# The inverse norms of q leave for DRAM in runs of 128 bytes, the planner's times for DRAM trips are set anew, and squares and scores may also use other pairs of a chunk

## The chip, the cores and the metric

The kernel runs on one core of one Trainium2 chip. The metric is the time of the whole program on the device, in microseconds: 2173.47 us as the median of three runs (2170.49 to 2175.32). TensorE (PE) multiplies matrices, VectorE (DVE), ScalarE (ACT) and GpSimd (POOL) work on elements, SyncE (SP) issues all DMAs from one queue.

## The reference

```python
# B, N, C = 4, 6080, 256; d_ff = 2048; all float32
qn = q / (np.linalg.norm(q, axis=1, keepdims=True) + 1e-6)     # over the 6080 tokens
kn = k / (np.linalg.norm(k, axis=1, keepdims=True) + 1e-6)
s = kn.transpose(0, 2, 1) @ qn / tau                           # 256 x 256 per batch
a = softmax(s, -1)                                             # sum + 1e-9
x = (v @ a).reshape(B * N, C)
h = x @ w_in
g = h * (1.0 / (1.0 + np.exp(-1.702 * h)))
out = g @ w_out
```

## The kernel before

Attention over channels needs only a 256 x 256 matrix per batch, and it is folded into the first weights: `a.T`-weighted `w_in` is made once per batch, and v goes through it directly. Float32 products are made of three matmuls with operands split into a high and a low part (ACT copies the high part, DVE subtracts to get the low one).

The main work is cut into 4 batches x 6 chunks of 1024 tokens (one chunk of each batch has 960) x 8 pairs of 128-wide feature blocks, 192 pairs in all. A pair (`lay`) has seven products `m1` to `m7` into `ps_x`, `ps_y`, `ps_z` (L818), copies and sums on ACT and DVE (L852 to L861), the gate on ACT (L872), its high and low parts (L877, L881), and the second product into `ps_o` (L894).

Beside the pairs of batch b runs the attention of batch b + 1, in small jobs. For each unit of 2 x 128 tokens a `score_job` loads q and k, splits them (L308, L313), multiplies (L388), sums on DVE (L406) and squares and adds for the norms (L321 on ACT, L333 on POOL). A `square_job` only loads again and squares: the four units of batch 1 whose scores were made at the start need it. When all units are done, `softmax_job` runs one chain:

- `norms_blocks`, `norms_part` (DVE, L413, L417), then to DRAM and back with channels on partitions (`part_rows`, L423; `quarters`, L429);
- `norms_sum`, `norms_root` (POOL), `norms_b` (DVE): the inverse norms `rn`, 128 x 4, q in the first two columns;
- q's two columns to DRAM as a row `q_row` (L445), and the row back, broadcast to 128 partitions, as `rq` (L452);
- `softmax_a` (DVE, L500, L504): x from sums, rn and rq, and its extreme; the exponential on ACT (L509); the scaling, a transposition and a trip through DRAM that turns x (`turned`, L533; `whole`, named `mixed` in the trace, L539); then the products with `w_in` (`fold`, L610) and the splitting of the new weights (L702, L704), which the first pair of batch b + 1 needs.

The order on every engine is set while the program is built. A planner goes through the pairs with its own clock (a matmul triple is 1.0 of its units, which is 0.68 us). It keeps for each token the time at which it is ready, and gives a job's step a place on its engine once what it needs is ready by that clock. A DMA costs nothing on SP; its `wait=` is the time until its data count as there. So `wait=` decides behind how much other work the reader of the data stands in its engine's queue. Each engine then runs its own list in order and waits on semaphores: an instruction whose data are late holds up all behind it.

Of the kernel before, what the change touches and what calls it, by code (L numbers as in the profile page):

```python
# [11 lines left out]
F32 = mybir.dt.float32  # L12
# [7 lines left out]
P = 128  # L20
# [8 lines left out]
def channel_attention_then_glu(  # L29
# [23 lines left out]
    nc = tc.nc  # L53
    B, N, C = q.shape
    DFF = w_in.shape[1] // 2
    NC2 = C // P
# [25 lines left out]
    small = ctx.enter_context(tc.tile_pool(name="small", bufs=1))  # L82
# [116 lines left out]
    class Attention:  # L199
# [223 lines left out]
            nc.sync.dma_start(self.part_rows, self.part_sums)  # L423

        def norms_in(self):
            self.quarters = small.tile([P, 2 * NC2, P // 32], F32, tag="quarters", name="quarters")
            src = self.part_rows.rearrange("(a u) (n b) -> b u n a", u=32, b=P // 32)
            for b in range(P // 32):
                nc.sync.dma_start(self.quarters[32 * b : 32 * b + 32], src[b])  # L429

        def norms_sum(self):
            self.rn = small.tile([P, 2 * NC2], F32, tag="rn", name="rn")
            nc.vector.tensor_reduce(self.rn, self.quarters, axis=AX.X, op=ALU.add)

        def norms_root(self):
# [2 lines left out]
        def norms_b(self):  # L438
            rn = self.rn
            nc.vector.tensor_scalar_add(rn, rn, 1e-6)  # L440
            nc.vector.reciprocal(rn, rn)

        def norms_q_out(self):
            self.q_row = dram.tile([1, C], F32, name=f"q_row{self.b}")
            nc.sync.dma_start(self.q_row.rearrange("o (n p) -> p (o n)", p=P), self.rn[:, :NC2])  # L445

        def norms_k(self):
            nc.vector.tensor_scalar_mul(self.rn[:, NC2:], self.rn[:, NC2:], rtau)
# [258 lines left out]
    whole = {}  # L707
# [96 lines left out]
    class Hidden:  # L804
# [54 lines left out]
        def add(self, out, a, z):  # L859
            out, a, z = (getattr(self, t) for t in (out, a, z))  # L860
            nc.vector.tensor_tensor(out, a, z, op=ALU.add)  # L861
# [65 lines left out]
    PAIRS = NF // 2  # L927
# [442 lines left out]
    def turn(tag, token, releases, deep=2):  # L1370
        ring = rings.setdefault(tag, [])
        deps = list(ring[-deep][1]) if len(ring) >= deep else []
        if ring and ring[-1][0] != token:
            deps.append(ring[-1][0])
        ring.append((token, releases))
        return deps
# [88 lines left out]
    def mix_room(s):  # L1465
        for n in range(4):
            mix_rooms[s, n] = turn("words", ("mix", s, n, "load"), [("mix", s, n, "keep")])
# [58 lines left out]
    def v_job(b, c, due, begin):  # L1526
        job = Job(due, begin)
        key = ("v", b, c)
        pair = (b * NCHUNK + c) * PAIRS
        for second in range(2):  # L1530
            low = ((*key, "px"), (*key, "py")) if not second else ((*key, "pw"), (*key, "pz1"))
            room = turn("words", (*key, second), [low[0], (*key, second, "+", 1)])
            room += turn("words", (*key, second), [low[1], *([(*key, "pz0")] if second else [])])
            job.add("SP", 0, (*key, second), room, v_load, b, c, second, wait=6.0 if b or c > 1 else 9.5)
            for n in range(3 if second else 2):
                deps = [(*key, second, "+", n - 1)] if n else [(*key, second)]
                job.add(
                    *(("DVE", 1.15) if (b, c) == (0, 1) else ("POOL", 2.2)),
                    (*key, second, "+", n), deps, v_sum, b, c, second, n,
                )  # L1540
            last = [(*key, second, "+", 2 if second else 1)]
            if second:
                job = Job(due - 0.5, begin)
                maker[*key, "late"] = job
                parts = (("pw", None, 1.0, 1.15), ("pz", 0, 1.0, 1.15), ("pz", 1, 1.0, 1.15))
            else:
                parts = (("px", None, 1.65, 1.9), ("py", None, 1.65, 1.9))
            for tag, n, da, dd in parts:
                name = tag if n is None else f"{tag}{n}"
                deps = list(last)  # L1550
                if second and (b or c):
                    deps += [("m4" if tag == "pw" else "m3", pair - 1)]
                if tag in ("px", "py") and (b, c) == (0, 1):
                    deps += [("s1", 7)]
                if not second and (b, c) >= (0, 2):
                    deps += [("m6", pair - PAIRS - 1)]
                job.add("ACT", da, (*key, name, 0), deps, v_part, b, c, tag, n, False)
                job.add("DVE", dd, (*key, name), [(*key, name, 0)], v_part, b, c, tag, n, True)
# [56 lines left out]
    def softmax_job(b, begin):  # L1615
        A = ats[b]
        job = Job(begin + 3, begin)
        key = ("soft", b)

        def add(eng, dur, name, deps, fn, *a, **kw):  # L1620
            job.add(eng, dur, (*key, name), deps, fn, *a, **kw)

        last = [summed[b, i] for i in range(2)]
        room = turn("sq", (*key, "blocks"), [(*key, "part")])
        add("DVE", 1.05, "blocks", [*last, *room], A.norms_blocks)
        add("DVE", 1.05, "part", [(*key, "blocks")], A.norms_part)
        job.add("SP", 0, (*key, "out"), [(*key, "part")], A.norms_out, wait=3.5)
        job.add("SP", 0, (*key, "in"), [(*key, "out")], A.norms_in, wait=5.0)
        add("DVE", 0.3, "sum", [(*key, "in")], A.norms_sum)
        add("POOL", 1.5, "root", [(*key, "sum")], A.norms_root)  # L1630
        add("DVE", 0.6, "b", [(*key, "root")], A.norms_b)
        job.add("SP", 0, (*key, "qo"), [(*key, "b")], A.norms_q_out, wait=3.5)
        add("DVE", 0.3, "k", [(*key, "b")], A.norms_k)
        room = turn("sq", (*key, "q"), [(*key, "x")])
        job.add("SP", 0, (*key, "q"), [(*key, "qo"), *room], A.norms_q, wait=3.5)
        room = turn("qs", (*key, "x0"), [(*key, "out2")])
        add("DVE", 1.6, "x0", [(*key, "q"), ("sums", b, len(A.units)), *room], A.softmax_a, 0)
        add("DVE", 1.6, "x", [(*key, "x0")], A.softmax_a, 1)
        maker[*key, "exp"] = job
        add("ACT", 5.8, "exp", [(*key, "x")], A.softmax_b)  # L1640
        add("DVE", 1.8, "c", [(*key, "exp")], A.softmax_c)
        add("DVE", 1.05, "tblocks", [(*key, "c")], A.turn_blocks)
        job.add("SP", 0, (*key, "out2"), [(*key, "tblocks")], A.turn_out, wait=5.0)
        room = turn("qs", (*key, "whole"), [("mixed", b)])
        job.add("SP", 0, (*key, "whole"), [(*key, "out2"), *room], A.turn_in, wait=4.0)
        add("ACT", 1.0, "turn", [(*key, "whole")], A.turned)
        job.add("DVE", 1.15, ("turned", b), [(*key, "turn")], A.turned_low)
        for n in range(4):
            add("DVE", 0.45, ("mix", n), [(*key, ("mix", n - 1)) if n else ("turned", b)], A.mixed, n)
        used = [("fold", b, NG // 2 - 1, len(FOLD) - 2)]  # L1650
        room = turn("sq", (*key, ("mix", "h")), used) + turn("sq", (*key, ("mix", "h")), used)
        add("ACT", 1.0, ("mix", "h"), [(*key, ("mix", 3)), *room], A.mixed_split, False)
        job.add("DVE", 1.15, ("mixed", b), [(*key, ("mix", "h"))], A.mixed_split, True)
# [160 lines left out]
    for b in range(B):  # L1814
        for c in range(NCHUNK):
            if b or c:
                p = (b * NCHUNK + c) * PAIRS
                v_job(b, c, p - (4 if b else 1), p - 5)
            if b == 0 and c in MIX_AT:
                mix_room(MIX_AT.index(c))  # L1820
        if b + 1 < B:
            o = b * NCHUNK * PAIRS
            u, last_u = ats[b + 1].direct, len(ats[b + 1].units)
            again = list(range(u))
            for p in range(3 if b else PAIRS + 1, TOTAL):
                if b == 0 and p % PAIRS == 0 and p // PAIRS in MIX_AT:
                    mix_job(MIX_AT.index(p // PAIRS), p)
                if p % PAIRS == 5 and again or u == last_u:
                    square_job(b + 1, again.pop(0), o + p)
                elif p % PAIRS not in (0, 5):  # L1830
                    score_job(b + 1, u, o + p)
                    u += 1
                    if u == last_u:
                        half_job(Job(o + p + 2, o + p + 1), b + 1, u, [])
                if u == last_u and not again:
                    break
            softmax_job(b + 1, o + p)
            for h in range(NG // 2):
                weight_job(b + 1, h, o + NCHUNK * PAIRS - PAIRS + (-4, 1)[h])
# [42 lines left out]
```

## Time and profile before

| | us |
|---|---|
| median of three runs | 2173.47 |
| the profiled execution | 2173.61 |
| its span | 2171.8 |
| PE busy | 2148.0 (99%) |
| ACT busy | 1543.3 (71%) |
| DVE busy | 1328.0 (61%) |
| POOL busy | 439.0 (20%) |

The span is what the trace covers; 1.8 us of the execution lie around it. Matmuls overlap in the records: one of 128x512 lasts 0.39 us, and the next starts 0.227 us after it when the granted clock is full.

### The profile page before, as it was taken

To read this page: it belongs to the slowest core of one execution; us is meant where nothing else is said; L and a number is where in the kernel's file an instruction comes from. 1 tells how busy PE (TensorE), PEld (TensorE's weight loads), DVE (VectorE), ACT (ScalarE), POOL (GpSimd) and SP (SyncE) were. 2 spreads that over 40 slices of the span, in tenths; PEclk is the share of its full clock that TensorE was granted. 3 is DMA by queue.
4 is the path that set the end of the run, shared out by engine and by line. 5 is a ranking of instruction groups with operands and counts; after the bars stand their busy time and mean duration, and the time that the engine had idled before them with its cause. 6 is when DMAs were issued, how large, how long until landed. Compare 5 with 4: busy or idle time off the path is not lost.

```text
span 2171.8 us, 26774 instructions
## 1 busy us (share of the span) xinstructions
PE 2148.0 (99%) x9654; PEld 1791.5 (82%) x9654; DVE 1328.0 (61%) x1996; ACT 1543.3 (71%) x2740; POOL 439.0 (20%) x465
## 2 busy tenths in 40 slices
PE   9999999999999999998999999999899999999999
PEld 8888888887888888887888888888788888888887
DVE  7986656656666666665566666666556644544443
ACT  7987777776677777775667777777566766666665
POOL 0003234231212423321121332242112100100100
PEclk9999999999999999999999999999999999999999
DMA  9433334212322222221222212121222110110100
GB/s 368 163 108 92 122 97 155 92 42 69 107 86 88 63 78 63 85 66 45 93 88 85 81 59 78 49 90 61 51 88 87 59 39 20 59 39 20 56 20 19
DMA packets 104757, 175.46 MB, mean 81 GB/s; under 512 B 22832, under 2 KB 31664, under 8 KB 104624
## 3 DMA queue, kind: packets, MB, share of 16 engines
q1 hardware_dynamic: 104624, 173.76, 24.5%
q8 instruction: 75, 1.23, 0.2%
q14 instruction: 58, 0.48, 0.1%
HBM read 137.52 MB, written 36.20 MB: 80 GB/s over the span
## 4 chain that ended last, share of the span: by engine, by line
PE 94%; DMA 3%; ACT 1%; DVE 1%; issue 0%; SPq 0%; POOL 0%; DVEq 0%; ACTq 0%
PE ps_o L894 46%; PE ps_x L818 23%; PE ps_z L818 11%; PE ps_y L818 6%; PE s L388 4%; PE s L349 2%; PE ps_w L610 1%; DMA q_row<-rn 1%; DMA rq<-q_row 1%; DMA words<-in_w_in 0%; PE ps_w L663 0%; DMA part_rows<-part 0%; DVE gl L881 0%; DVE r L861 0%; DMA quarters<-part_rows 0%
## 5 line engine op out<-in xcount | busy, mean ns | idle before, releaser
L894 PE MATMUL ps_o<-gh,wo_l 128*128 128x512 f32 (+1 forms) x1536 | 596.2, 388 | 0.0
L894 PE MATMUL ps_o<-gh,wo_h 128*128 128x512 f32 (+1 forms) x1536 | 596.2, 388 | 0.0
L894 PE MATMUL ps_o<-gl,wo_h 128*128 128x512 f32 (+1 forms) x1536 | 472.0, 388 | 0.8 <-DVE gl L881 0.8
L881 DVE TENSOR_TENSOR gl<-g,gh 128x512 fp32r<-128x512 f32 (+1 forms) x384 | 273.9, 753 | 145.1 <-ACT gh L877 144.9
L894 PEld LDWEIGHTS ps_o<-gl,wo_h 128*128 128x128 f32 x1536 | 289.0, 188 | 58.8 <-DVE gl L881 1.2
L894 PEld LDWEIGHTS ps_o<-gh,wo_h 128*128 128x128 f32 x1536 | 289.2, 188 | 57.9
L894 PEld LDWEIGHTS ps_o<-gh,wo_l 128*128 128x128 f32 x1536 | 289.1, 188 | 57.6
L333 POOL TENSOR_TENSOR acc<-acc,sq 128x256 f32<-128x256 f32 x276 | 219.3, 801 | 521.8 <-ACT sq L321 510.9
L818 PE MATMUL ps_x<-vh,wh 128*128 128x512 f32 (+1 forms) x768 | 300.4, 391 | 16.6 <-DVE r L861 15.9
L881 DVE TENSOR_TENSOR gl<-ps_y,gh 128x512 fp32r<-128x512 f32 (+1 forms) x192 | 131.7, 686 | 294.3 <-ACT gh L877 293.8
L818 PE MATMUL ps_x<-vl,wh 128*128 128x512 f32 (+1 forms) x768 | 299.0, 389 | 0.0
L818 PE MATMUL ps_x<-vh,wl 128*128 128x512 f32 (+1 forms) x768 | 298.1, 388 | 0.0
L783 POOL TENSOR_TENSOR v_raw<-v_raw 128x512 f32<-128x512 f32 (+1 forms) x110 | 159.8, 1461 | 633.4 <-DMA v_raw<-in_vT 365.0
L872 ACT ACTIVATE r<-r 128x512 f32<-128x512 f32 (+1 forms) x192 | 120.5, 628 | 191.4 <-DVE r L861 191.4
L852 ACT COPY r<-ps_x 128x512 f32<-128x512 f32 (+1 forms) x189 | 110.3, 583 | 178.6 <-PE ps_x L818 178.5
L877 ACT CAST gh<-g 128x512 fp32r<-128x512 f32 (+1 forms) x384 | 216.4, 613 | 0.1
L881 DVE TENSOR_TENSOR gl<-r,gh 128x512 fp32r<-128x512 f32 (+1 forms) x192 | 146.9, 765 | 66.7 <-ACT gh L877 63.7
L818 PEld LDWEIGHTS ps_x<-vh,wh 128*128 128x128 f32 x768 | 145.1, 189 | 47.1 <-DVE r L861 17.7
L852 ACT COPY r<-ps_z 128x512 f32<-128x512 f32 (+1 forms) x192 | 111.9, 583 | 80.2 <-PE ps_z L818 80.2
L818 PEld LDWEIGHTS ps_x<-vh,wl 128*128 128x128 f32 x768 | 144.9, 189 | 29.1
L818 PEld LDWEIGHTS ps_x<-vl,wh 128*128 128x128 f32 x768 | 145.2, 189 | 25.8
L406 DVE TENSOR_TENSOR sums<-sums,s 128x256 f32<-128x256 f32 x138 | 58.0, 420 | 153.6 <-PE s L388 151.2
(145 smaller groups left out, 3304.0 us busy)
## 6 DMA issues: line engine op xcount, KB each, us to landing
v_raw<-in_vT SPq DMA_DIRECT2D x80, 512.0 KB, 4.6
out_T<-osb SPq DMA_DIRECT2D x80, 256.0 KB, 2.0
raw_q<-in_q SPq DMA_DIRECT2D x74, 256.0 KB, 2.7
raw_k<-in_k SPq DMA_DIRECT2D x74, 256.0 KB, 2.7
fold<-t SPq DMA_DIRECT2D x48, 256.0 KB, 2.8
fold<-b SPq DMA_DIRECT2D x36, 256.0 KB, 2.9
v_raw<-in_vT SPq DMA_DIRECT2D x16, 480.0 KB, 3.9
words<-in_w_in SPq DMA_DIRECT2D x8, 512.0 KB, 5.4
```

Of the source, the lines that this page charges most:

```text
L333: nc.gpsimd.tensor_tensor(acc, acc, sq[:, j, :], op=ALU.add)
L349: nc.tensor.matmul(self.s[:, i, :], lhsT=lhsT, rhs=rhs, start=self.first, stop=last, skip_group_check=True,)
L388: nc.tensor.matmul(out, lhsT=ks[:, j, low, ci], rhs=rhs, start=n == 0, stop=n == len(terms) - 1, skip_group_check=True,)
L406: nc.vector.tensor_tensor(out, out, part, op=ALU.add)
L610: nc.tensor.matmul(self.ps, lhsT=l, rhs=r, start=n == 0, stop=n == 2)
L783: eng.tensor_tensor(out, a, z, op=ALU.subtract)
L818: nc.tensor.matmul(out, lhsT=l[:, wi, :], rhs=r[:, n, : self.hw], start=first and m == 0, stop=last and m == 2, skip_group_check=True,)
L852: nc.scalar.copy(r, getattr(self, src))
L872: nc.scalar.activation(g, source, AF.Gelu_apprx_sigmoid)
L877: nc.scalar.copy(gh, g)
L881: nc.vector.tensor_tensor(gl, g, gh.bitcast(F32), op=ALU.subtract)
L894: nc.tensor.matmul(out[d][:, : self.hw], lhsT=l[:, at_f, d * P : (d + 1) * P], rhs=r, start=first and l is wo[0] and r is gh, stop=last an ...
```

## The change

`norms_in` makes a tile `wide` of 128 x 2 x 32 and clears its first half on POOL; the inverse norms are its first four columns. A new step on DVE transposes it in blocks of 32 x 32, which puts the norms of 32 channels side by side on one partition, and `q_row` is written by four DMAs of 2 rows x 32 elements (128 bytes a run) in place of one DMA of 128 x 2 single elements. Five `wait=` values of the chain grow. Counted from 0: the attention jobs of batches 2 and 3 now use pair 5 of each chunk for scores too; those of batch 1 may use pair 0 of a chunk, beside pair 5, for squares alone, and pair 5 for scores once the squares are done. The preparation of v for chunks 3 to 5 of batch 0 is due three pairs earlier.

```diff
         def norms_in(self):
+            self.wide = small.tile([P, 2, 32], F32, tag="wide", name="wide")
+            nc.gpsimd.memset(self.wide[:, 0], 0.0)
...
-            self.rn = small.tile([P, 2 * NC2], F32, tag="rn", name="rn")
+            wide = self.wide[:, 0]
+            self.rn = wide[:, : 2 * NC2]
...
+        def norms_rows(self):
+            nc.vector.transpose(self.wide[:, 1], self.wide[:, 0])
+
         def norms_q_out(self):
             self.q_row = dram.tile([1, C], F32, name=f"q_row{self.b}")
-            nc.sync.dma_start(self.q_row.rearrange("o (n p) -> p (o n)", p=P), self.rn[:, :NC2])
+            to = self.q_row.rearrange("o (n a v) -> a (o n) v", n=NC2, v=32)
+            for a in range(P // 32):
+                nc.sync.dma_start(to[a], self.wide[32 * a : 32 * a + NC2, 1])
...
-        job.add("SP", 0, (*key, "qo"), [(*key, "b")], A.norms_q_out, wait=3.5)
+        add("DVE", 0.3, "rows", [(*key, "b")], A.norms_rows)
+        job.add("SP", 0, (*key, "qo"), [(*key, "rows")], A.norms_q_out, wait=5.5)
...
-        job.add("SP", 0, (*key, "q"), [(*key, "qo"), *room], A.norms_q, wait=3.5)
+        job.add("SP", 0, (*key, "q"), [(*key, "qo"), *room], A.norms_q, wait=11.0)
...
-                v_job(b, c, p - (4 if b else 1), p - 5)
+                v_job(b, c, p - (4 if b or c > 2 else 1), p - 5)
...
-                if p % PAIRS == 5 and again or u == last_u:
+                if p % PAIRS in (0, 5) and again or u == last_u:
                     square_job(b + 1, again.pop(0), o + p)
-                elif p % PAIRS not in (0, 5):
+                elif p % PAIRS:
                     score_job(b + 1, u, o + p)
```

The other three waits go from 5.0 to 8.5 (`in`), 5.0 to 9.0 (`out2`) and 4.0 to 9.5 (`whole`).

The order on DVE in the softmax of batch 1 (batches, chunks and pairs are counted from 0; pairs 36 and 37 of 192, one `r<-ps_x,r` per pair) before, from the inverse norms to the first use of rq:

```order
L441 RECIPROCAL rn<-rn 128x4
L448 TENSOR_SCALAR rn<-rn,rtau 128x2
L800 TENSOR_TENSOR vl<-v_raw,vh 128x2x480
L881 TENSOR_TENSOR gl<-ps_y,gh 128x512
L861 TENSOR_TENSOR r<-ps_x,r 128x512
L861 TENSOR_TENSOR ps_z<-ps_z,r 128x512
L406 TENSOR_TENSOR sums<-sums,s 128x256 x2
L881 TENSOR_TENSOR gl<-r,gh 128x512
L500 SCALAR_TENSOR_TENSOR x<-sums,rn,rq 128x256
```

The same stretch of DVE's order now:

```order
L447 STREAM_TRANSPOSE wide<-wide 128x32
L456 TENSOR_SCALAR wide<-wide,rtau 128x2
L406 TENSOR_TENSOR sums<-sums,s 128x256 x2
L808 TENSOR_TENSOR vl<-v_raw,vh 128x2x480
L889 TENSOR_TENSOR gl<-ps_y,gh 128x512
L869 TENSOR_TENSOR r<-ps_x,r 128x512
L869 TENSOR_TENSOR ps_z<-ps_z,r 128x512
L889 TENSOR_TENSOR gl<-r,gh 128x512
L889 TENSOR_TENSOR gl<-g,gh 128x512 x2
L406 TENSOR_TENSOR sums<-sums,s 128x256 x2
L508 SCALAR_TENSOR_TENSOR x<-sums,wide,rq 128x256
```

The first use of rq moved behind `gl<-g,gh` of the pair and behind a second `sums`, so two sums of consecutive pairs now lie between the norms and it.

SP's order at the same place before, and then now (`fold` is a load of weights, `v_raw` one of v, `mixed` the way back of the turned x):

```order
L593 DMA fold<-b_0_426 128x512 x2
L593 DMA fold<-b_0_431 128x512 x2
L423 DMA part_rows_4592<-part 128x16
L429 DMA quarters<-part_rows_4592 32x16x1 x4
L445 DMA q_row_4679<-rn 128x2x1
L452 DMA rq<-q_row_4679 128x256
L768 DMA v_raw<-in_vT 128x2x480 x2
L533 DMA turned_4939<-x 32x8x32 x8
L539 DMA mixed<-turned_4939 128x2x256
```

```order
L601 DMA fold<-b_0_426 128x512 x2
L423 DMA part_rows_4522<-part 128x16
L431 DMA quarters<-part_rows_4522 32x16x1 x4
L601 DMA fold<-b_0_431 128x512 x2
L453 DMA q_row_4668<-wide 2x32 x4
L776 DMA v_raw<-in_vT 128x2x480 x2
L460 DMA rq<-q_row_4668 128x256
L541 DMA turned_4944<-x 32x8x32 x8
L917 DMA out_T<-osb 128x512
L547 DMA mixed<-turned_4944 128x2x256
```

The two loads of v moved from behind the load of rq to ahead of it, and one store of the output ahead of `mixed`.

DVE's order in the softmax of batch 2, where the norms stood in pair 83 before and stand in pair 79 now; first before, then now (`osb` is the output's copy at the start of a chunk):

```order
L441 RECIPROCAL rn<-rn 128x4
L448 TENSOR_SCALAR rn<-rn,rtau 128x2
L881 TENSOR_TENSOR gl<-r,gh 128x480
L881 TENSOR_TENSOR gl<-g,gh 128x480 x2
L800 TENSOR_TENSOR vl<-v_raw,vh 128x1024
L406 TENSOR_TENSOR sums<-sums,s 128x256 x2
L500 SCALAR_TENSOR_TENSOR x<-sums,rn,rq 128x256
```

```order
L447 STREAM_TRANSPOSE wide<-wide 128x32
L456 TENSOR_SCALAR wide<-wide,rtau 128x2
L808 TENSOR_TENSOR vl<-v_raw,vh 128x480 x3
L406 TENSOR_TENSOR sums<-sums,s 128x256 x2
L889 TENSOR_TENSOR gl<-ps_y,gh 128x480
L869 TENSOR_TENSOR r<-ps_x,r 128x480
L869 TENSOR_TENSOR ps_z<-ps_z,r 128x480
L889 TENSOR_TENSOR gl<-r,gh 128x480
L912 COPY osb<-ps_o 128x512 x4
L889 TENSOR_TENSOR gl<-g,gh 128x480 x2
L406 TENSOR_TENSOR sums<-sums,s 128x256 x2
L508 SCALAR_TENSOR_TENSOR x<-sums,wide,rq 128x256
```

The use of rq moved from the norms' own pair into the next one; the place in batch 3 (norms in pair 131 before, 127 now) moved in the same way.

## Rows read from the trace of the kernel before

**Rows 1.** The page's busy times: us, share of the span, instructions.
```profile
PE 2148.0 (99%) x9654; PEld 1791.5 (82%) x9654; DVE 1328.0 (61%) x1996; ACT 1543.3 (71%) x2740; POOL 439.0 (20%) x465
```
**Rows 2.** Waits: engine, line, waited for; us in total, times, longest us.
```profile
PE ps_x L818 <- DVE r L861: 15.9, 3, 6.8
...
DVE sums L406 <- PE s L388: 151.2, 55, 3.0
...
DVE x L500 <- DMA rq<-q_row: 25.4, 3, 8.9
```
**Rows 3.** The chain of work that ended last: start us, us, what.
```profile
476.26 8.45 DMA q_row<-rn
484.78 5.85 DMA rq<-q_row
...
978.12 1.40 PE s L388 x8
989.27 1.38 PE s L388 x8
...
1533.70 8.74 DMA q_row<-rn
1542.49 6.36 DMA rq<-q_row
```
**Rows 4.** Timeline, softmax of batch 1: start us, us, instruction, [idle before, releaser].
```profile
490.73 0.49 DVE L500 SCALAR_TENSOR_TENSOR x<-sums,rn,rq 128x256 f32<-128x256 f32 x1 [8.15 <-DMA rq<-q_row]
...
491.18 0.39 PE L894 MATMUL ps_o<-gh,wo_l 128*128 128x512 f32 x1
...
496.04 0.80 PE L818 MATMUL ps_x<-vh,wh 128*128 128x512 f32 x1 [2.98 <-DVE r L861]
...
502.36 0.39 PE L894 MATMUL ps_o<-gh,wo_h 128*128 128x512 f32 x1
```
**Rows 5.** Timeline of PE, softmax of batch 2.
```profile
1005.70 0.59 PE L894 MATMUL ps_o<-gl,wo_h 128*128 128x480 f32 x2
1012.48 0.77 PE L818 MATMUL ps_x<-vh,wh 128*128 128x480 f32 x1 [6.19 <-DVE r L861]
...
1017.45 0.39 PE L818 MATMUL ps_x<-vh,wh 128*128 128x480 f32 x1
```
**Rows 6.** Timeline of PE, softmax of batch 3.
```profile
1543.71 0.59 PE L894 MATMUL ps_o<-gl,wo_h 128*128 128x480 f32 x2
1551.06 0.77 PE L818 MATMUL ps_x<-vh,wh 128*128 128x480 f32 x1 [6.76 <-DVE r L861]
...
1557.04 0.38 PE L894 MATMUL ps_o<-gh,wo_h 128*128 128x480 f32 x1
```
**Rows 7.** Stretches: PE, PEld, DVE, ACT, POOL busy us (instructions), granted clock, DMA share, GB/s.
```profile
959.86:971.46 11.60, 11.60 (x55) 9.84 (x54) 8.67 (x13) 9.16 (x18) 2.31 (x3) 1.00 0.40 131
...
1004.00:1016.00 12.00, 5.81 (x20) 4.64 (x19) 4.88 (x7) 3.14 (x6) 2.93 (x3) 0.78 0.28 100
```
**Rows 8.** DMA issues: number, KB each, median us from issue to landing.
```profile
v_raw<-in_vT SPq DMA_DIRECT2D x16, 480.0 KB, 3.9
...
turned<-x SPq DMA_DIRECT2D x24, 32.0 KB, 1.6
```
**Rows 9.** Timeline of SP's DMA issues, softmax of batch 1.
```profile
513.13 3.79 SPq L533 DMA_DIRECT2D turned<-x  x8
518.33 0.38 SPq L539 DMA_DIRECT2D mixed<-turned  x1
```
**Rows 10.** Groups by form: count, busy us, mean ns of one, idle before.
```profile
L406 DVE TENSOR_TENSOR sums<-sums,s 128x256 f32<-128x256 f32 x138 | 58.0, 420 | 153.6 <-PE s L388 151.2
...
L800 DVE TENSOR_TENSOR vl<-v_raw,vh 128x960 fp32r<-128x960 f32 x8 | 9.2, 1151 | 0.0
...
L413 DVE STREAM_TRANSPOSE blocks<-acc 128x512 f32<-128x512 f32 x3 | 2.1, 702 | 0.0
...
L440 DVE TENSOR_SCALAR rn<-rn 128x4 f32<-128x4 f32 x3 | 0.5, 164 | 1.1 <-POOL rn L436 1.1
```

More of the change, by code (lines that the diff above doesn't have):

```diff
@@ L1627, in softmax_job @@
         job.add("SP", 0, (*key, "out"), [(*key, "part")], A.norms_out, wait=3.5)
-        job.add("SP", 0, (*key, "in"), [(*key, "out")], A.norms_in, wait=5.0)
+        job.add("SP", 0, (*key, "in"), [(*key, "out")], A.norms_in, wait=8.5)
         add("DVE", 0.3, "sum", [(*key, "in")], A.norms_sum)
@@ L1642, in softmax_job @@
         add("DVE", 1.05, "tblocks", [(*key, "c")], A.turn_blocks)
-        job.add("SP", 0, (*key, "out2"), [(*key, "tblocks")], A.turn_out, wait=5.0)
+        job.add("SP", 0, (*key, "out2"), [(*key, "tblocks")], A.turn_out, wait=9.0)
         room = turn("qs", (*key, "whole"), [("mixed", b)])
-        job.add("SP", 0, (*key, "whole"), [(*key, "out2"), *room], A.turn_in, wait=4.0)
+        job.add("SP", 0, (*key, "whole"), [(*key, "out2"), *room], A.turn_in, wait=9.5)
         add("ACT", 1.0, "turn", [(*key, "whole")], A.turned)
```

## The prediction

> **What bounds the kernel now.** I read the page's busy times first. PE is busy 2148.0 of 2171.8 us [rows 1], so nothing that runs beside PE can give time back unless PE waits for it. The waits, read next, say where it does: three waits of `ps_x` for DVE's `r`, 15.9 us in total, and almost nothing else; and DVE's `x` waits three times for the load of `rq`, 25.4 us [rows 2]. The chain of waits joins the two. At each softmax it leaves PE for two DMAs in a row: the write of `q_row`, 8.45 us to 8.74 us, and the load of `rq`, 5.85 us to 6.36 us [rows 3] (the first and the last of three places). DVE stands on `x` because `rq` is not there, the sums and gates queued behind `x` are late, ACT is late with them, and PE runs dry.
>
> What a stop costs PE is more than the idle time, as the timeline of PE shows. Batch 1: between 491.18 and 502.36 eighteen starts fit at 0.227 us each, 4.09 us; they took 11.18, so 7.1 us are lost [rows 4]. Batch 2: from 1005.70 to 1017.45 there are 14 matmuls of 480 columns, 0.217 us each at full clock, 3.04 us; they took 11.75, so 8.7 are lost [rows 5]. Batch 3: from 1543.71 to 1557.04 there are 17 matmuls, 3.69 us; they took 13.33, so 9.6 are lost [rows 6]. Not all of it is idleness (2.98, 6.19 and 6.76 us before `ps_x` in the same rows); 2.5 us or more at each place is the clock: the granted clock falls to 0.78 over the stretch with the stop, against 1.00 elsewhere [rows 7], and for some 5 us after the stop matmuls start 0.40 to 0.43 us apart, PE's 1.2 GHz level in place of 2.4. **The three stops together: 25.4 us.** That is all that this change can win: the same matmuls are issued afterwards, in the same number.
>
> **The change part by part.**
>
> The write of `q_row`. Now it takes 8.45 to 8.74 us for 256 single elements [rows 3]. Afterwards it is a transposition of 128x32 on DVE and four DMAs of two 128-byte runs. The transposition: 0.2 us, between an operation on 128x4 (164 ns) and a transposition of 128x512 (702 ns) [rows 10]. The four DMAs: the trace has no such write to q_row, but `turned` also leaves SBUF for DRAM in runs of 128 bytes, 256 runs in each DMA, and lands 1.6 us after its issue [rows 8]. Eight of them are issued in 3.79 us, 0.47 each, and the DMA that waits for all of them is issued 5.20 us after the first [rows 9]; four less 0.47 each makes 3.3 us. Bounds: 1.6 us (one such DMA, if issues overlapped) and 8.74 + 3 x 0.47 = 10.2 us (if each write still cost what it costs now). I take 3.3, the nearest row by run length and direction. This saves 5 us of a chain that is late by 8.15 to 8.9: alone it would not be enough.
>
> A page speaks against this: the Trainium skill, "DMA: Bandwidth & Descriptors", section Specifications, says that transfers below 512 bytes make the DMA engine read, modify and write, and 128 bytes are below that like 4. By that rule the write would not get cheaper, and the sum would end at the upper bound; the trace disagrees in part, since `turned` shows 128-byte runs landing in 1.6 us [rows 8].
>
> The place of `x`. The planner's two waits for this trip go from 3.5 + 3.5 to 5.5 + 11.0 of its units (0.68 us each), so from 4.8 to 11.2 us, and the order shows the result. Before, `x` stood in the same pair as the norms; now a whole pair lies between. In that pair DVE's `sums` waits for PE's score block, and score blocks come one pair apart, 11.15 us (978.12 to 989.27 [rows 3]), a little more where the pair has 512 columns. So `x` cannot start earlier than 11.2 us after the write of `q_row` is issued, and the data need 0.2 + 3.3 + 6.4 = 9.9 us. Batches 2 and 3: `rq` is there 1.3 us or more before `x`. No stop, and no clock loss: 8.7 + 9.6 = 18.3 us won.
>
> Batch 1 is tighter, because SP now issues the two loads of v ahead of `rq`, and the second waits until DVE has done `vl`, which stands behind `sums`. Counted from the start of that `sums`: 0.84 (two of 420 ns) + 1.15 (`vl`) [rows 10] + some 0.5 for the issue of a load (`turned` takes 0.47 each); `rq` is issued at 2.5 and lands at 8.9 if the loads of v do not disturb it, or at 12.8 if it waits out a load of v, 3.9 us [rows 8]. `x` stands behind the next `sums`, so it starts at 11.15 + 0.84 = 12.0. At worst DVE is 0.8 us late, and it has idle time to take that up: it waits 2.7 us before such a sum (151.2 / 55 [rows 2]). I put 0.7 us on PE for this place, and win 6.4.
>
> What else moves. The clearing of `wide` on POOL is one small operation ahead of the root, in time that POOL spends waiting; in batch 1 and 3 it stands right behind the last squares, which the chain needs anyway: 0. Norms that arrive a pair later would push the softmax back, and so would the longer waits `in`, `out2` and `whole`; against that the score jobs end two pairs earlier for batch 1 and five for batches 2 and 3, since pair 5 of each chunk is used. In the order the first split of new weights moves from pair 45 to 44, from 91 to 89 and from 139 to 137, and they are needed at 48, 96 and 144. So nothing on the way to the next batch gets late: 0. The price of using more pairs is a fuller ACT: a pair with scores and squares comes seven times in a chunk instead of six. Such pairs stand in long rows already: in the ten pairs from 855 to 971 us PE is busy all of 11.60 us in each at full clock, and ACT 9.16 us at most [rows 7] (the row shown is the last of the ten). A pair of the new order has no more ACT work than the fullest before: 0.
>
> **Sum.** 2173.6 (the profiled execution; the median of the runs is 2173.5) - 18.3 - 6.4 = 2148.9, so **2149 us**.
>
> **Rivals.**
>
> - *The write stays slow* (the rule above). Then `q_row` needs 10.2 and the data 0.2 + 10.2 + 6.4 = 16.8 us against 11.2 to 14: `x` is 3 to 5 us late at each place. Before, 8.15 to 8.9 us of lateness cost 7.1 to 9.6, so this costs some 3 to 5 each, 9 to 15 in all: 2157 to 2163, say 2160. For it: the length is the same for both in that rule. Against: `turned`.
> - *The loads of v take the place of the wait at batch 1.* If the second load finds its room late, or `rq` queues behind both loads (7.8 us instead of 3.9), `x` is 4.7 us late there, and that place costs some 5 us with the clock: 2153 to 2154. For it: SP issues in order, and `v_raw` is now ahead. Against: the room was planned to be free.
> - *The wait goes on to the next trip.* `mixed` now stands behind a store of the output that waits for DVE. If ACT meets the turned matrix late, it holds up PE as `x` did, at one place or more: 8 us each, 2157 to 2165. Against: ACT's conversion of it stands more than a pair behind the transposition, and `turned` to `mixed` took 5.20 us [rows 9].
> - *Slower: ACT falls behind in the dense rows.* The place is the run of score pairs in chunks of batches 1 and 2 that are no longer broken by a pair 5 without scores, and pairs 22 to 24. If ACT's 9.16 us of work cannot be kept within 11.6 because its pieces wait on PE and DVE in turn, each such pair ends late, PE idles for about 1 us and may run the next 5 us at the lower clock, 2.5 us more: 3.5 us a pair. From eight such pairs on the 25 us are eaten; at a dozen the time is 2149 + 42 = 2191. Against: PE waited in none of the dense pairs before [rows 2, 7].
>
> **How the numbers follow.** Chances: forecast 0.73, slow write 0.08, loads of v 0.10, next trip 0.05, dense pairs 0.04. The forecast's own range is 2146 to 2152: the three runs of before lie up to 3 us from their median, and the losses are read to about 1 us. The range of 8 in 10 reaches up to the loads of v and the near end of the slow write and the next trip, so 2145.5 to 2158; lower than 2145.5 would need time that no wait shows. A change of 0.2%, 4.3 us, is about what a measurement of this kernel can tell from none. Faster than that, below 2169.1: all cases but the dense pairs and a little of the two that lose more at several places, 0.92. Same: 0.03, from two or three places lost again. Slower: 0.05, the dense pairs and something that I do not see.
>
> **What would show it.** Right: the waits have no line of PE for DVE's `r` over 1 us; DVE's `x` waits for `rq` less than 1 us at batches 2 and 3; from the first issue of `q_row` to that of `rq` 3 to 4 us at batches 2 and 3; the granted clock stays at 1.00 around 490, 980 and 1500 us. Wrong in its size: `q_row` still 8 us or more, with `x` waiting. Wrong in kind: waits of PE for ACT or for a score's `qs` and `ks` in the dense chunks, or for `aT` and `wl` before pairs 48, 96 and 144.

## The result and the profile after

The kernel after takes 2148.78 us (median of five runs, 2148.36 to 2149.43) against 2172.70 us for the kernel before in the same session (five runs, 2170.49 to 2175.32): ratio 0.9891, 95% interval 0.9876 to 0.9905. The forecast was 2149.0 us. The profiled execution took 2149.34 us with a span of 2147.5.

The page's busy times of after, which answer to [rows 1]:

```profile
PE 2139.3 (100%) x9654; PEld 1784.8 (83%) x9654; DVE 1326.4 (62%) x1999; ACT 1544.5 (72%) x2740; POOL 444.8 (21%) x468
```

PE has the same 9654 matmuls, and 8.2 us of its span are not busy, against 23.8 before. Its busy time is 8.7 us shorter with the same matmuls. That is the lower clock after each stop, which lengthens matmuls and so counts as busy: the mean granted clock was 0.994 in before and is 0.999 in after. 15.6 + 8.7 = 24.3 us, the whole change of the span.

The waits of after (for [rows 2]), the longest of PE's and the one of DVE that answers:

```profile
PE ps_y L927 <- DVE ones L104: 1.0, 1, 1.0
PE ps_b L493 <- ACT diag L489: 0.6, 1, 0.6
...
DVE sums L406 <- PE s L388: 147.2, 56, 3.0
```

No wait of PE for `r` is left that is worth a line, and DVE's `x` never waits for `rq`. SP's DMA issues of after at the three softmaxes (start us, us, what; [rows 3] has the same trip before):

```profile
473.39 1.16 SPq L453 DMA_DIRECT2D q_row<-wide  x4
474.90 3.32 SPq L776 DMA_DIRECT2D v_raw<-in_vT  x2
478.45 0.34 SPq L460 DMA_DIRECT2D rq<-q_row  x1
...
952.18 1.16 SPq L453 DMA_DIRECT2D q_row<-wide  x4
954.29 0.35 SPq L460 DMA_DIRECT2D rq<-q_row  x1
...
1480.62 1.16 SPq L453 DMA_DIRECT2D q_row<-wide  x4
1482.73 0.35 SPq L460 DMA_DIRECT2D rq<-q_row  x1
```

From the first issue of the write to the issue of the load, which waits for all four, 2.11 us pass at batches 2 and 3, where the write took 8.45 to 8.74 us before. The load is faster too, though nothing in it was changed (DMA issues of after: number, KB, median us to landing):

```profile
rq<-q_row SPq DMA_DIRECT2D x3, 128.0 KB, 3.3
```

It was 5.85 to 6.36 [rows 3]. DVE at the softmax of batch 1 after ([rows 4] before):

```profile
486.77 0.88 DVE L406 TENSOR_TENSOR sums<-sums,s 128x256 f32<-128x256 f32 x2 [0.32 <-PE s L388]
487.68 0.48 DVE L508 SCALAR_TENSOR_TENSOR x<-sums,wide,rq 128x256 f32<-128x256 f32 x1
488.20 0.42 DVE L512 TENSOR_REDUCE m<-x 128x1 f32<-128x256 f32 x1
```

`x` runs 14.3 us after the write was issued, and `rq` lies there from 481.9 on. The stretches around the three softmaxes and a long run of dense pairs in after (us, then busy us of PE, PEld, DVE, ACT, POOL, granted clock, DMA share, GB/s; [rows 7] before):

```profile
476.00:500.00 24.00, 24.00 (x109) 19.86 (x108) 15.15 (x22) 16.33 (x29) 4.18 (x3) 1.00 0.17 47
955.00:980.00 25.00, 25.00 (x116) 21.42 (x116) 17.35 (x28) 17.62 (x33) 2.88 (x2) 1.00 0.32 111
1483.00:1508.00 25.00, 25.00 (x117) 21.43 (x116) 16.53 (x27) 17.95 (x34) 2.88 (x2) 1.00 0.34 110
850.00:950.00 100.00, 100.00 (x457) 83.32 (x456) 63.34 (x96) 73.96 (x130) 30.89 (x37) 1.00 0.21 61
```

PE is busy all the time at full clock in all four; this run of dense pairs costs nothing.

### The profile page after: what moved, and what is told of

Same layout as the page of the kernel before. It is cut to its first block, busy times and chain, and to the rows that moved or that the text cites. A ratio compares the mean times of both kernels' runs of the same rounds, so it can differ in the third digit from the quotient of the medians.

```text
span 2147.5 us, 26790 instructions
## 1 busy us (share of the span) xinstructions
PE 2139.3 (100%) x9654; PEld 1784.8 (83%) x9654; DVE 1326.4 (62%) x1999; ACT 1544.5 (72%) x2740; POOL 444.8 (21%) x468
## 4 chain that ended last, share of the span: by engine, by line
PE 96%; DMA 2%; ACT 1%; DVE 1%; issue 0%; SPq 0%; ACTq 0%; DVEq 0%
PE ps_o L902 48%; PE ps_x L826 24%; PE ps_z L826 12%; PE ps_y L826 6%; PE s L388 4%; DMA raw_k<-in_k 1%; PE ps_w L618 1%; PE ps_w L671 0%; DMA words<-in_w_in 0%; DMA words<-in_w_out 0%; ACT z L134 0%; ACT wf L688 0%; ACT eighths L136 0%; ACT g L880 0%; ACT vh L810 0%
## 5 line engine op out<-in xcount | busy, mean ns | idle before, releaser
L889 DVE TENSOR_TENSOR gl<-g,gh 128x512 fp32r<-128x512 f32 (+1 forms) x384 | 282.2, 774 | 142.9 <-ACT gh L885 142.7
L333 POOL TENSOR_TENSOR acc<-acc,sq 128x256 f32<-128x256 f32 x276 | 227.1, 829 | 507.8 <-ACT sq L321 497.0
L880 ACT ACTIVATE g<-ps_x 128x512 f32<-128x512 f32 (+1 forms) x192 | 114.1, 594 | 50.7 <-PE ps_x L826 50.4
```

The lines of the kernel that those rows point to most:

```text
L333: nc.gpsimd.tensor_tensor(acc, acc, sq[:, j, :], op=ALU.add)
L880: nc.scalar.activation(g, source, AF.Gelu_apprx_sigmoid)
L889: nc.vector.tensor_tensor(gl, g, gh.bitcast(F32), op=ALU.subtract)
```

## The experiments

The change has three parts: the write, the waits and the pair rules (the use of pairs 0 and 5, with v's due time; these were only moved together, so what each of them does is not shown). The prediction said that the write alone would not be enough and that the waits move `x`. Runs with each part present or absent test both; beside each, before ran on the same chip. In the sessions of the first eight its median was 2169.0 to 2169.1 us (7 runs each), 3.6 us less than beside after; beside the last four it ran once each (2168.1 to 2169.6 us).

### The old write in the kernel after

```diff
-            to = self.q_row.rearrange("o (n a v) -> a (o n) v", n=NC2, v=32)
-            for a in range(P // 32):
-                nc.sync.dma_start(to[a], self.wide[32 * a : 32 * a + NC2, 1])
+            nc.sync.dma_start(self.q_row.rearrange("o (n p) -> p (o n)", p=P), self.rn[:, :NC2])
```

> The changed kernel with the old write of q_row: one DMA of 256 single elements; the new waits, pairs and the transposition stay (its result is not used). In the changed kernel q_row was under way 2.1 us and rq 3.3 us; x came 13.8 to 14.3 us after the first issue of q_row. Theory A (the load of rq is slow because the row was written in single elements): write 8.4, load 6.4, together 14.8, so x waits 0.5 to 1.0 us at each place and PE loses under 1 us at each: 2149 to 2152. Theory B (the load was slow because the loads of v were issued right behind it; here none is at batches 2 and 3): 8.4 + 3.3 = 11.7, x does not wait: 2148 to 2149.5. Rival from the prediction (the cheaper write is what won the time): x waits 5 us or more, 2160.

Measured: 2148.93 us, ratio to before 0.9910 [0.9895, 0.9924]. SP's issues at batch 2 of this kernel:

```profile
950.75 0.39 SPq L451 DMA_DIRECT2D q_row<-wide  x1
958.53 0.33 SPq L458 DMA_DIRECT2D rq<-q_row  x1
```

The write is about as slow as in before, 7.8 us here and 8.1 and 8.8 at the other batches, and `x` does not wait. With the other two parts there, the new write gives nothing, and the rival from the prediction falls. The load of `rq`:

```profile
rq<-q_row SPq DMA_DIRECT2D x3, 128.0 KB, 4.9
```

It took 4.5 to 5.4 us, where after, which differs in the write alone, had 3.2 to 3.5: neither the 6.4 of theory A nor the 3.3 of theory B.

### The new write alone

The kernel before, with the change's `wide`, `norms_rows` and four DMAs, old waits and pair rules.

> The kernel before with the new write alone (transposition and four DMAs of 128-byte runs); old waits, old pairs, and the loads of v right behind rq as before. x has a slot 6.3 to 6.5 us after the norms. The prediction said that the write alone saves 5 of 8.5 us and is not enough: x late by 3 us, PE loses 3 to 5 us at each place, 2158 to 2164. Theory A (the load follows the way the row was written): 0.2 + 2.1 + 3.3 = 5.6 us, x is not late: 2148 to 2151. Theory B (the loads of v behind it slow it): 0.2 + 2.1 + 6.4 = 8.7, x waits 2.3 us, 2153 to 2158.

Measured: 2148.57 us, 0.9908 [0.9892, 0.9925]. SP and DVE at batch 1 of this kernel, from two timelines:

```profile
477.36 1.20 SPq L453 DMA_DIRECT2D q_row<-wide  x4
479.62 0.35 SPq L460 DMA_DIRECT2D rq<-q_row  x1
480.09 7.72 SPq L776 DMA_DIRECT2D v_raw<-in_vT  x2
```
```profile
483.32 0.48 DVE L508 SCALAR_TENSOR_TENSOR x<-sums,wide,rq 128x256 f32<-128x256 f32 x1 [0.36 <-DMA rq<-q_row]
```

`x` keeps its old place, some 6 us behind the write (before, DVE stood at `x` at 490.73 - 8.15 = 482.58, 6.3 us after 476.26 [rows 3, 4]). The trip needs 2.26 + 3.7 us and just fits: one wait of 0.36 us. So the write alone is enough, though with nothing to spare; theory A has the time right, and the load's 3.7 us is nearer to its 3.3 than to 6.4.

### The pair rules alone

The kernel before with the change's three lines on pairs and v's due time.

> The kernel before with the pair rules alone (squares and scores also in other pairs, the preparation of v due earlier); old write, old waits. The order shows x at the same place as in the changed kernel, right behind the last sums, so the longer waits are not what moved it. The write takes 8.4 us. Theory A: the load 6.4, x waits 0.5 to 1.0 us: 2149 to 2152. Theory B: 3.3 at batches 2 and 3, x does not wait: 2148 to 2149.5. The prediction's step that the waits set the place of x would give the stops of before: 2172.

Measured: 2149.51 us, 0.9912 [0.9897, 0.9927]. SP and DVE at batch 1:

```profile
472.20 0.37 SPq L445 DMA_DIRECT2D q_row<-rn  x1
479.95 0.33 SPq L452 DMA_DIRECT2D rq<-q_row  x1
```
```profile
486.73 0.48 DVE L500 SCALAR_TENSOR_TENSOR x<-sums,rn,rq 128x256 f32<-128x256 f32 x1
```

The slow write is there (7.75 us), the waits are the old ones, and `x` comes 14.5 us after the write, as in after: the units are done earlier, so the norms leave a pair ahead of the last `sums`, and `x` stands behind that. The load of `rq` took 4.4 to 6.2 us. So the pair rules alone are enough too.

### The write and the waits, without the pair rules

The kernel after with the old three lines on pairs and v's due time.

> The changed kernel with the old pair rules: new write, new waits. The norms come at the old time, the chain after them is planned some 15 us longer, and the order shows the last split of the first new weights in pair 47, right ahead of pair 48 that needs it (44 to 45 in the changed kernel). Theory: x does not wait, but PE stands ahead of pair 48 for the new weights, once or twice 1 to 4 us, little or nothing at batches 2 and 3 (pair 93 for 96): 2149 to 2155. Rival: the longer waits alone cost nothing, 2148 to 2149.5.

Measured: 2159.31 us, 0.9959 [0.9944, 0.9974]: 10.5 us over after. The place, the new weights of batch 1, was expected; a loss of this size was not. `x` does not wait. What PE waits for (us in total, times, longest):

```profile
PE ps_z L826 <- DVE wl L710: 2.6, 2, 1.9
PE ps_x L826 <- ACT ps_y L865: 2.0, 2, 1.8
PE ps_z L826 <- ACT wh L712: 1.7, 2, 0.9
```

PE's timeline gives the places, two of the first pairs with the new weights of batch 1, and a wait 6 us behind them:

```profile
587.92 0.50 PE L826 MATMUL ps_z<-vh,wh 128*128 128x512 f32 x1 [0.85 <-ACT wh L712]
...
589.38 0.56 PE L826 MATMUL ps_z<-vh,wl 128*128 128x512 f32 x1 [0.72 <-DVE wl L710]
...
636.97 0.50 PE L826 MATMUL ps_z<-vh,wh 128*128 128x512 f32 x1 [0.87 <-ACT wh L712]
...
639.60 0.50 PE L826 MATMUL ps_z<-vh,wl 128*128 128x512 f32 x1 [1.89 <-DVE wl L710]
...
646.22 0.50 PE L826 MATMUL ps_x<-vh,wh 128*128 128x512 f32 x1 [1.78 <-ACT ps_y L865]
```

Their idle times are 6.1 us. The rest is the clock, as at the stops before: PE is busy for 2145.4 us here with the same matmuls, 6.1 more than in after. Two of the stretches:

```profile
590.00:600.00 10.00, 10.00 (x40) 8.27 (x40) 6.43 (x10) 5.58 (x10) 3.54 (x4) 0.85 0.14 52
...
640.00:650.00 10.00, 8.21 (x25) 6.01 (x24) 4.31 (x7) 5.45 (x10) 5.00 (x7) 0.71 0.46 136
```

In DVE's order the first split of the new weights stands at pair 47 here, at 45 in before and at 44 in after, and pair 48 needs it. Here it starts just as PE comes to wait for it; in after (second line) it starts some 27 us earlier:

```profile
588.64 0.68 DVE L710 TENSOR_TENSOR wl<-wf,wh 128x512 fp32r<-128x512 f32 x1
```
```profile
561.56 1.70 DVE L710 TENSOR_TENSOR wl<-wf,wh 128x512 fp32r<-128x512 f32 x2
```

The longer waits pushed the softmax and all behind it back, and the pair rules had been paying for that.

### One wait back, the waits out, the waits alone

Three runs on what the waits are worth. First the kernel of the last run with a single number put back:

```diff
-        job.add("SP", 0, (*key, "q"), [(*key, "qo"), *room], A.norms_q, wait=11.0)
+        job.add("SP", 0, (*key, "q"), [(*key, "qo"), *room], A.norms_q, wait=3.5)
```

> The kernel with the new write, the new waits and the old pair rules (2159.3 us), with one number back: the wait of the load of q's norms, 11.0, is 3.5 again; 8.5, 5.5, 9.0 and 9.5 stay. Theory A (this one wait sends x a pair later and the splits of the new weights with it, and those splits cost the 10.5 us): no wait of TensorE for the new weights, 2148.7 us. Theory B (the waits of the turned trip, 9.0 and 9.5, cost it): still about 2159 us.

Measured: 2148.34 us, 0.9906 [0.9890, 0.9923], and PE waits for no new weights: theory A. At batch 1 `x` stands 7.1 us behind the write again (15.8 in the last kernel), and the first split at pair 45. The 10.5 us hang on the wait of this load, with the others in place. This kernel also shows the load of `rq` behind the new write with two loads of v issued right ahead of it (batch 2):

```profile
990.67 2.06 SPq L776 DMA_DIRECT2D v_raw<-in_vT  x2
992.90 0.34 SPq L460 DMA_DIRECT2D rq<-q_row  x1
```
```profile
rq<-q_row SPq DMA_DIRECT2D x1, 128.0 KB, 4.6
```

The kernel before this one has 4.5 us at the same place, where after, with no load of v ahead, has 3.2 at batch 3. Then the kernel after with all five old waits:

> The kernel after with the five waits of the plan put back to 5.0, 3.5, 3.5, 5.0 and 4.0; the new write and the pair rules stay. Theory A (the write and the place of x do all the work, the waits none): x stands in the same pairs as after, no stop of TensorE at the softmax, 2148.7 us, within 1 us of after. Theory B (the longer waits are what keeps the trips after the softmax, the turned product and mixed, out of TensorE's way): one or more stops of 1 to 4 us at mixed or at the new weights, 2152 to 2160 us.

Measured: 2148.84 us, 0.9907 [0.9892, 0.9922]. The waits give nothing: write and pair rules do the same without them. And the kernel before with the five new waits alone:

> The kernel before with the five longer waits alone; write in single elements, old pair rules. Theory A (the waits push x a pair later, which is room enough for the slow trip of 7.8 + 6 us, and push the new weights of batch 1 to the pair that needs them, as in the kernel with write and waits): no wait of x, the two stops near 590 and 640 us, 2159 us. Theory B (the slow trip still ends after x, so both costs add up): x waits for the load again and the time is 2165 to 2185 us.

Measured: 2160.84 us, 0.9962 [0.9947, 0.9977]. Neither theory is right as it stood. The new weights come late as above, and `x`, though a pair later, still waits at batches 2 and 3; DVE's and PE's timelines of batch 3:

```profile
1547.82 1.30 DVE L500 SCALAR_TENSOR_TENSOR x<-sums,rn,rq 128x256 f32<-128x256 f32 x1 [3.69 <-DMA rq<-q_row]
```
```profile
1552.20 0.48 PE L818 MATMUL ps_x<-vh,wh 128*128 128x480 f32 x1 [1.32 <-DVE r L861]
```

A wait of 3.69 us at `x` left PE idle for 1.32 us here, and one of 1.69 at batch 2 for none; 8.15 to 8.9 had left it idle for 2.98 to 6.76 [rows 4 to 6].

### What the slow write is made of

The kernel with the pair rules alone, and a second write of the same single elements to an unread row ahead of the first:

```diff
+            self.q_dup = dram.tile([1, C], F32, name=f"q_dup{self.b}")
+            nc.sync.dma_start(self.q_dup.rearrange("o (n p) -> p (o n)", p=P), self.rn[:, :NC2])
```

> The kernel before with the pair rules alone (2149.5 us), and the single-element write doubled: 256 more single elements go to a second, unread row just ahead. With the pair rules alone, write to issue of the load is 7.8 to 8.1 us, the load 4.8, and x starts 14.5 us after the write, so some 2 us are to spare. Theory A (the single elements are what the trip's time consists of and they are worked off one after another): write to load some 15.5 us, x waits 5 to 6 us at each of three softmaxes, TensorE stops some 2.5 us each (x's wait less the 3.2 us that TensorE had in hand before, 8.5 less 5.3) and loses 4 to 5 us each with its clock, 2162 us (2156 to 2172). Theory B (the trip's time is a fixed price of a DRAM trip, whatever the number of elements): write to load stays near 8 to 9 us, 2149.5 us.

Measured: 2149.75 us, 0.9911 [0.9896, 0.9926]; no wait of `x`. Median landings, and the issues at batch 2:

```profile
q_dup<-rn SPq DMA_DIRECT2D x3, 1.0 KB, 8.1
q_row<-rn SPq DMA_DIRECT2D x3, 1.0 KB, 7.9
```
```profile
952.45 0.47 SPq L447 DMA_DIRECT2D q_row<-rn  x1
962.81 0.33 SPq L454 DMA_DIRECT2D rq<-q_row  x1
```

At batches 1 and 3 twice the elements took the same time: the two went side by side. At batch 2 the second write took 10.2 us and the first 8.6. Nowhere was it the 15.5 us of theory A, which falls; theory B's 8 to 9 us do not hold at batch 2 either. The DMA view of before, from 476 to 486 us, shows where there is room (40 slices of 0.25 us, busy tenths of the engines and what they moved):

```profile
DMA  0000230000000000000000000000000000000000
GB/s 0 0 0 0 2 2 0 0 0 0 0 0 0 0 0 0 0 0 0 0 0 0 0 0 0 0 0 0 0 0 0 0 0 0 0 0 0 0 0 0
DMA packets 272, 0.00 MB, mean 0 GB/s; under 512 B 272, under 2 KB 272, under 8 KB 272
```

The packets are through the engines by 477.5, and nothing moves in this view in the 7 us until the write lands at 484.7. The next run put four unread writes at once behind the new one, in four layouts.

> The kernel after, and at each of the three writes of q's norms four further writes of the same 256 numbers to rows that nothing reads, each timed by its own landing: single elements side by side, as before wrote them; single elements 128 bytes apart; single elements 512 bytes apart; single elements side by side, in four transfers of 64. In the trace of before and of the kernel with the doubled write, the 272 packets of the write pass through the transfer engines within about 0.5 us, and nothing moves in the 7 us until it lands; and two such writes to two rows took 7.9 and 8.1 us side by side, no longer than one. Theory A (elements that fall into the same stretch of DRAM are written one after another there): side by side about 8 us, 128 bytes apart and 512 bytes apart 2 to 3 us, four transfers about 8 us, since they go to the same stretch. Theory B (the 256 elements of one transfer are confirmed one after another, wherever they lie): side by side, 128 and 512 bytes apart all about 8 us, four transfers about 2 to 3 us each. Theory C (a transfer with packets of 4 bytes has this price, however it is laid out or cut): all four about 8 us. The time of the kernel is expected within 2 us of after, since x has some 9 us to spare there.

Measured: 2159.05 us in its one run, and landings of 8.2 to 9.8 us for all four. That looks like theory C, but the four went one behind another, and a landing may have waited for the one ahead, so it decides nothing. Nor did the time stay within 2 us: SP stood behind the extra writes for 10.4 us before stores of the output, the load of `rq` took 7.2 us at batch 1, where `x` waited 4.3 us for it, and PE waited 3.6 us for output buffers and 3.1 for `r`. So three more runs wrote one kind at a time, with a load of it right behind whose issue marks the landing:

```diff
+            rows, run = {1: (32, 1), 2: (128, 2), 3: (128, 8)}[self.b]
+            q_try = dram.tile([rows, run], F32, name=f"q_try{self.b}")
+            nc.sync.dma_start(q_try, self.wide[:rows, 1, :run])
+            back = small.tile([P, 16], F32, tag="back", name="back")
+            nc.sync.dma_start(back[:rows, :run], q_try)
```

> The kernel after, with one further write to a row of DRAM and a small load of it right behind, after the load of q's norms, one kind for each batch: batch 1 writes 32 packets of 4 bytes, batch 2 128 packets of 8 bytes, batch 3 128 packets of 32 bytes. What is read is the time from the issue of that write to the issue of its load, alone in its queue, which the kernel with four writes at once could not give. Nearest rows: 256 packets of 4 bytes 7.8 to 8.7 us, 8 packets of 128 bytes in four transfers 2.1 us, and in before the write of part_rows, 128 packets of 64 bytes, 1.5 us. Theory C (a fixed price for a write in packets of 4 bytes, not for their number): batch 1 some 7.5 us; batch 3 1.5 to 2 us; batch 2 tells where the price ends. Theory D (the price is for the number of packets, each small one some 0.03 us): batch 1 about 2 us, batches 2 and 3 about 4.5 us. The load behind stands in the queue's way for up to 8 us, so the kernel's time may rise by up to 10 us by either theory and tells nothing here.

> As the run before, with other kinds of packets: batch 1 writes 128 packets of 64 bytes, batch 2 8 packets of 4 bytes, batch 3 128 packets of 4 bytes. Theory C (fixed price for packets of 4 bytes): batch 1 1.5 to 2 us, batch 2 and batch 3 both some 7.5 us. Theory D (price by the number of packets): batch 1 about 4.5 us, batch 2 about 1.6 us, batch 3 about 4.5 us. The time of the kernel tells nothing here.

> As the two runs before, each batch's further write now 128 packets of 4 bytes that lie apart in DRAM: 32 bytes apart at batch 1, 512 at batch 2, 64 at batch 3. Side by side 128 packets of 4 bytes took 7.1 us, 32 of them 4.4, 8 of them 2.1, and 128 packets of 32 or 64 bytes 2.9 and 3.0. Theory E (packets that fall into the same short stretch of DRAM are written one after another): 512 bytes apart some 3 us, as a packet of 64 bytes, and 32 and 64 bytes apart between that and 7.1 us. Theory F (each packet of 4 bytes has its price wherever it lies): all three about 7 us. The time of the kernel tells nothing here.

SP's issues at batches 2 and 3 of the second of these runs (8 and 128 packets of 4 bytes, side by side):

```profile
954.08 0.31 SPq L463 DMA_DIRECT2D q_try<-wide  x1
956.22 0.26 SPq L465 DMA_DIRECT2D back<-q_try  x1
...
1482.57 0.42 SPq L463 DMA_DIRECT2D q_try<-wide  x1
1489.67 0.32 SPq L465 DMA_DIRECT2D back<-q_try  x1
```

and at batch 2 of the third (128 packets of 4 bytes, 512 bytes apart):

```profile
954.24 0.42 SPq L463 DMA_DIRECT2D q_try<-wide  x1
956.94 0.32 SPq L465 DMA_DIRECT2D back<-q_try  x1
```

| packets | layout in DRAM | us from issue to the next |
|---|---|---|
| 8 x 4 bytes | side by side | 2.14 |
| 32 x 4 bytes | side by side | 4.39 |
| 128 x 4 bytes | side by side | 7.10 |
| 128 x 4 bytes | 32 bytes apart | 3.11 |
| 128 x 4 bytes | 64 bytes apart | 2.65 |
| 128 x 4 bytes | 512 bytes apart | 2.70 |
| 128 x 8 bytes | side by side | 3.92 |
| 128 x 32 bytes | side by side | 2.85 |
| 128 x 64 bytes | side by side | 3.03 |

Each is one sample with the load of `rq`, issued 0.4 us ahead, in flight; at batch 1 (32 x 4 bytes, 32 bytes apart, 128 x 64 bytes) two loads of v are in flight as well. That load lands 3.2 to 3.5 us after its issue in after, so the times from 2.65 to 3.11 us are upper bounds: with no load of `rq` ahead, `part_rows`, 128 packets of 64 bytes, took 1.43 us at batch 2 of after. Theory C falls with the first two rows, and D with the last two (2.85 and 3.03 where it had 4.5). Theory E has the best of it, and F (7 us wherever they lie) falls: the same 128 packets of 4 bytes cost 7.1 us side by side and at most 2.7 us when 64 bytes apart, both at batch 3. How long the stretch is within which packets hold each other up is not settled. The three kernels took 2148.86, 2148.66 and 2148.81 us in one run each: even 7 us more on SP behind `rq` cost nothing.

## Why the prediction was right, and where it was not

- *What the change could win.* Right. Three stops of 7.1, 8.7 and 9.6 us, 25.4 in all, were to be had; 23.9 came between the medians, 24.3 between the profiled spans. Reading the lost time off PE's start times, clock included, and not off the idle time alone (15.9 us), made the size right. On the chips of the experiments, where before took 2169.0 to 2169.1 us, the write alone and the pair rules alone won 20.5 and 19.5 us, so the ceiling itself differs by some 4 us from session to session.
- *The write.* Right in kind, a third too dear: 2.1 us, not 3.3. Most of the error, 0.7 of 1.2 us, were the issues: the four are out in 1.16 us, 0.29 each, where the eight of `turned` take 0.47 each. The transposition was 0.2 us as said. The upper end of 10.2 us did not occur. (The sum of the rival that starts from it, 16.8 us against 11.2 to 14, makes `x` 2.8 to 5.6 us late, not 3 to 5; nothing hangs on it.) The rule (the Trainium skill, "DMA: Bandwidth & Descriptors", section Specifications: below 512 bytes an engine reads, modifies and writes) has 4 and 128 bytes on the same side. The runs above show that this does not make their price the same: below 512 bytes the size and the layout of the packets made 2.1 to 8.7 us of it. Whether an engine read and modified anything, no run here shows.
- *"Alone it would not be enough".* Wrong: the write alone gave 2148.57 us. The step that failed is the load of `rq`, taken at 6.4 us from [rows 3] as if nothing but its issue time would change. It fell to 3.7 with the new write alone and to 3.3 in after; with only the old write put back into after it was 4.5 to 5.4. So it depends on the write ahead of it, and also on the v loads beside it: behind the new write, with two of them issued right ahead, it was 4.5 and 4.6. With 3.7 the trip takes 6.0 us and fits the slot that `x` always had. What in the write slows the load was not tried, and once, behind the slowest write of the doubled kernel (10.2 us), it took 3.1, so the cause stays open. How much PE would have lost with a load of 6.4 us is not shown either: in the kernel with the waits alone it ran through a wait of `x` of 1.69 us.
- *What moves `x`.* Wrong in the cause, right in the place. The waits can move it by a pair (the waits alone do), but the pair rules do so too, and with them the waits change nothing: put back, they gave 2148.84 us. The 11.2 us at least that the prediction counted were 13.8 to 14.3.
- *The loads of v at batch 1.* The mechanism was there (the v loads are issued between write and load, and `rq` leaves 5.1 us after the write instead of 2.1), but `rq` lay ready at 481.9 and `x` came at 487.7: nothing of the 0.7 us put there was lost. The rival that they take the wait over did not occur.
- *"Nothing on the way to the next batch gets late: 0."* Right for the sum, since the order of after has the splits a pair earlier. But the two terms behind that zero are 10 us each way: the waits without the pair rules, and of them the one of the load of `rq`, cost 10.5 us at the new weights, and the pair rules took it back.
- *The slower rival, ACT behind in dense pairs.* Did not occur: PE was busy for 100.00 of 100 us from 850 on, at full clock.

So the time was right because the win had a ceiling, the three stops, and several ways reach it. The write alone, the pair rules alone and the three parts together all end at 2148.6 to 2149.5 us, and no version tried is clear of after. In this the number was lucky: it would have come out with the waits left as they were, so it does not bear out what the prediction said moves `x`.

## What to carry to other kernels

Price a stop by the start times of the bound engine up to where its full pace returns; and where a part of a change is said to be not enough, compare need and slot with both durations free, since the step behind a slow one may be slow because of it. When several parts aim at one stop, the stop is the ceiling and any one may reach it: build each alone before crediting one. A planner's longer wait protects the reader and delays all that follows it; look at the first user at the far end, here the split of the new weights, not only at the reader.

## What the hardware showed that was not expected

- A write of 256 single 4-byte elements side by side keeps the transfer engines busy for 0.5 us and lands after 7.7 to 9.2 us (before and the kernels that write it once); one of 128 after 7.1 us. Two such writes to two rows landed together in the time of one at two of three places; at the third the second took 10.2 us. The same 128 packets land within 2.7 us when they lie 64 or 512 bytes apart, and 128 packets of 32 or 64 bytes within 2.9 and 3.0 us.
- The load behind such a write was slower than behind 128-byte runs, with one exception: 4.5 to 5.4 us against 3.2 to 3.5 in after, for the same 128 KB. Two loads of v issued right ahead of it made it 4.5 and 4.6 us behind 128-byte runs too.
- In the kernel with the waits alone PE ran on through a wait of `x` of 1.7 us, and idled for 1.3 us at one of 3.7.
